# Retention and gated product on one core: 54 matmuls in two halves each, and sums, masks and first products in another order

## The chip, the cores and the metric

One core of a Trainium2 chip. The metric is the time of one execution in microseconds (us). Each kernel is run several times, in rounds with the kernel before on the same chip. Most executions agree within about 1%; a run that is over 1.5% above the fastest of its kernel is called slow and is left out of ratios. A ratio is the mean time of one kernel's fast runs over the mean of the other's fast runs of the same rounds, so it is not quite the ratio of the medians quoted beside it.

## The reference

```python
def reference(q, k, v, w_in, w_out):          # q, k, v: (8, 8, 576, 64)
    scores = q @ k.T / sqrt(64)               # per batch and head
    ret = scores * where(i >= j, gamma[h] ** (i - j), 0)
    x = (ret @ v) -> reshaped to (4608, 512)
    h = x @ w_in                              # (512, 2048)
    g = h * cos(h)
    return g @ w_out                          # (2048, 512)
```

(Shortened; the result is float32, (4608, 512).)

## The kernel before

The tokens are worked through in ten tiles of 512, 256, 256 and seven times 512 rows. In each tile TensorE first makes `h` ("first matmuls", `mm1`: 64 matmuls of 512 columns in tiles 4 to 9), ScalarE and VectorE turn it into `gT`, and then TensorE makes the output from `gT`. From tile 3 on the output is made with seven products instead of eight (Strassen's way), which needs sums `gs` of quarters of `gT`; VectorE (DVE) makes some, GpSimd (POOL) the others. Between these products stand small matmuls of the retention of the next tiles: scores (`sc`), states (`st`), and the parts `cross`, `own` and `same` of `ov`. The chain runs inside a tile: sums of `gs` on VectorE, then the addition `ot` that frees a PSUM bank, then the additions of the states (`s`, `carry`), then ScalarE's copy of the states to `sb`, then the cross matmuls `ov`, which read `sb`.

```python
def g_sum(n, x, e0, e1):
    # ... (which quarters, which operation: cut)
    on_dve = ...  # DVE takes 5, the second half of 2, and (6, first half) in tiles 4 to 8
    i = (nc.vector if on_dve else nc.gpsimd).tensor_tensor(
        out=tiles["gs", n, x][:, e0:e1], in0=i0, in1=i1, op=op_)
    if on_dve:
        tiles["gate"] = i
    elif "gate" in tiles:
        fence(i, tiles.pop("gate"), ...)     # GpSimd's sum waits for the last DVE sum

def sums_after(n, i):
    # ... (tile 3: cut)
    elif n <= CATCH and i in (3, 7):                 # tiles 4 to 7
        for x in (5, 2):
            g_sum(n, x, i - 3, i + 1)
        if i == 7:
            g_sum(n, 6, 0, 4)                        # the third DVE sum
        g_sum(n, 1, i - 3, i + 1)                    # GpSimd from here on
        if i == 7:
            for e in (0, 4):
                g_sum(n, 7, e, e + 4)
            g_sum(n, 6, 4, E2)

def mm2_seven(n, at):                                # the seven products of tiles 3 to 9
    for x in (3, 4, 5, 2, 1, 7, 6):
        # ... (retention of the next tiles at x == 5, 1 and 6: cut)
        parts = product(n, x)
        if x == 3:
            acts.append(lambda: nc.scalar.copy(u22, tiles["all", 3]))
        elif x == 4:
            add(u22, tiles["all", 4], u22)           # "ot": frees the bank of product 4
        # ...
```

## Time and profile before

| | before |
|---|---|
| time, median of 3 runs | 297.47 us (296.58 to 302.08) |
| span of the profiled run | 294.9 us, mean granted TensorE clock 1.0 |
| TensorE (PE) busy | 281.6 us, 95% |
| starts of the first matmuls of tiles 1, 3, 4 to 9 | 50.41, 83.91, 114.84, 145.65, 176.58, 205.96, 236.66, 264.98 us |

TensorE is the bound, so a change pays only where TensorE stands still. One measure is used throughout the rest, read from the trace: the **products stretch** of a tile, from the start of its last first matmul to the start of the next tile's first one. It holds the seven products and the retention matmuls between them, and all waits among these. Before, tiles 4 to 7 took 17.21, 17.34, 15.78 and 17.10 us; where nothing waits it is 15.7 to 15.9 us.

Some of TensorE's waits are put down to "issue": the profile shows nothing that it waits for. Beside them stands what this trace has of the instruction queue (line q8 of its page): 30 packets of 16,384 bytes, for 7,731 records of TensorE (loads, matmuls, its sequencer's), which is 258 records to a packet. The two longest issue waits stand at records 4801 and 6593, 7 x 256 apart. So 256 instructions of TensorE are called a "block" here, and the packet that ended last before TensorE went on is taken for the block's; both are inferred from these places, no line of the profile says so. At five places of this trace (packets ended at 106.18, 111.07, 174.60, 202.33 and 234.61 us) the first instruction behind the wait ran 1.3 to 1.5 us after the packet's end, and 3.4 to 5.2 us (once 8.0) after the first instruction of the block before.

### The profile page before, as it was taken

How to read it: one execution, taken by the hardware profiler on the slowest of the kernel's cores; microseconds unless marked ns; L12 is line 12 of the kernel's file. 1: busy time of each engine (PE TensorE's matmuls, PEld its weight loads, DVE VectorE, ACT ScalarE, POOL GpSimd, SP SyncE). 2: the span in 40 equal slices, each digit the busy share in tenths (PEclk: the TensorE clock that was granted, in tenths of full speed). 3: DMA queues.
4: the chain of work that ended last, by engine and by line, in shares of the span. 5: the costliest groups of instructions: out<-in, count | busy, mean ns of one | idle time of the engine just before them, and what ended most of it. 6: DMA issues, size and time to landing. Idle time of an engine off the chain costs nothing.

```text
span 294.9 us, 8852 instructions
## 1 busy us (share of the span) xinstructions
PE 281.6 (95%) x3850; PEld 190.9 (65%) x3850; DVE 208.0 (71%) x268; ACT 147.8 (50%) x197; POOL 176.7 (60%) x158
## 2 busy tenths in 40 slices
PE   7889999999999999998999979999999899999995
PEld 2568645748568886466746864588458754884594
DVE  5676656576759985788758865797579858945873
ACT  5646434625346545654376526734674567525620
POOL 7482047581192299698497784569566804870583
PEclk9999999999999999999999999999999999999999
DMA  7999999999999998999999999979942240021013
GB/s 217 261 171 194 219 247 251 177 302 235 205 224 215 197 201 205 188 214 175 202 224 232 177 221 203 236 184 218 203 119 39 76 109 0 4 87 57 0 38 108
DMA packets 119031, 50.39 MB, mean 171 GB/s; under 512 B 83024, under 2 KB 117968, under 8 KB 118992
## 3 DMA queue, kind: packets, MB, share of 16 engines
q1 hardware_dynamic: 114224, 45.10, 75.4%
q0 software_dynamic: 4224, 4.19, 8.8%
q8 instruction: 30, 0.49, 0.7%
q10 hardware_dynamic: 544, 0.52, 0.5%
q14 instruction: 9, 0.07, 0.1%
HBM read 36.70 MB, written 9.44 MB: 156 GB/s over the span
## 4 chain that ended last, share of the span: by engine, by line
PE 74%; DMA 9%; DVE 8%; ACT 2%; issue 2%; SPq 2%; POOL 2%; DVEq 0%; PEldq 0%; ACTq 0%
PE h L542 38%; PE o L694 23%; PE o L559 7%; DMA w_out_sb<-in_moe_w_out_dram 6%; PE ov L466 3%; DMA fv<-in_v_dram 3%; PE sc L283 2%; DVE gs L621 2%; DVE s L379 2%; DVE ot L719 2%; SPq L171 1%; DVE ret L295 1%; PE st L356 1%; POOL w_out_sb L965 1%; ACT sb L387 1%
## 5 line engine op out<-in xcount | busy, mean ns | idle before, releaser
L542 PE MATMUL h<-xT,w_in_sb 128*128 128x256 bf16 (+1 forms) x768 | 127.2, 326 | 0.9 <-DVE xT L491 0.8
L621 POOL TENSOR_TENSOR gs<-gT 128x1024 bf16<-128x1024 bf16 x42 | 88.2, 2129 | 62.3 <-DVE gs L621 31.0
L551 DVE TENSOR_TENSOR gT<-h,cosh 128x1024 bf16<-128x1024 f32 x72 | 88.0, 1223 | 46.3 <-ACT cosh L550 46.1
L550 ACT ACTIVATE cosh<-h,half_pi 128x1024 f32<-128x1024 f32 x72 | 80.2, 1114 | 56.2 <-PE h L542 56.2
L542 PEld LDWEIGHTS <-w_in_sb 128*128 128x128 bf16 x768 | 74.6, 98 | 50.8 <-DVE xT L491 1.6
L694 PEld LDWEIGHTS <-gs 128*128 128x128 bf16 x576 | 53.4, 98 | 10.6 <-issue 3.9
L180 POOL TENSOR_TENSOR qs<-fq,gq 128x512 bf16<-128x512 f32 x31 | 32.0, 1063 | 33.2 <-DMA fq<-in_q_dram 33.2
L694 PE MATMUL o<-ws,gs 128*128 128x256 bf16 (+1 forms) x352 | 39.4, 268 | 2.6 <-issue 2.6
L180 POOL TENSOR_TENSOR ks<-fk,gk 128x512 bf16<-128x512 f32 x32 | 34.4, 1090 | 6.1 <-DMA fk<-in_k_dram 5.9
L559 PE MATMUL o<-w_out_sb,gT 128*128 128x512 bf16 x128 | 30.5, 380 | 0.2 <-DMA w_out_sb<-in_moe_w_out_dram 0.2
L387 ACT CAST sb<-s 128x768 bf16<-128x768 f32 (+2 forms) x16 | 10.7, 672 | 34.6 <-DVE s L379 32.2
L719 DVE TENSOR_TENSOR ot<-o,ot 128x512 f32<-128x512 f32 (+2 forms) x32 | 19.7, 621 | 10.2 <-PE o L694 9.6
L694 PE MATMUL o<-w_out_sb,gs 128*128 128x256 bf16 x224 | 25.8, 273 | 0.6 <-DVE ot L719 0.6
L694 PE MATMUL o<-w_out_sb,gT 128*128 128x256 bf16 x224 | 25.8, 273 | 0.0
L491 ACT CAST xT<-ov 128x512 bf16<-128x512 f32 x26 | 15.4, 626 | 19.7 <-PE ov L466 19.7
L694 PEld LDWEIGHTS <-gT 128*128 128x128 bf16 x224 | 21.7, 98 | 4.0
L621 DVE TENSOR_TENSOR gs<-gT 128x1024 bf16<-128x1024 bf16 (+1 forms) x27 | 20.9, 810 | 0.4
L559 PEld LDWEIGHTS <-gT 128*128 128x128 bf16 x128 | 11.5, 98 | 12.7 <-issue 0.5
L719 DVE TENSOR_TENSOR ot<-ot,o 128x512 f32<-128x512 f32 x14 | 9.6, 687 | 7.5 <-ACT ot L749 6.1
L295 DVE TENSOR_TENSOR ret<-sc,tri 128x1024 bf16<-128x1024 f32 x12 | 14.6, 1214 | 0.0
L302 DVE TENSOR_TENSOR ret<-sc,tri 128x1024 bf16<-128x1024 f32 x9 | 10.7, 1219 | 1.8 <-PE sc L283 1.8
L466 PE MATMUL ov<-qT,sb 64*64 64x64 bf16 (+1 forms) x424 | 11.5, 201 | 0.5 <-ACT sb L387 0.2
(88 smaller groups left out, 193.8 us busy)
## 6 DMA issues: line engine op xcount, KB each, us to landing
out_dram<-ot SPq DMA_DIRECT2D x35, 256.0 KB, 3.9
fk<-in_k_dram SPq DMA_DIRECT2D x23, 256.0 KB, 6.7
fv<-in_v_dram SPq DMA_DIRECT2D x23, 256.0 KB, 4.9
fk<-in_k_dram SPq DMA_DIRECT2D x4, 512.0 KB, 7.6
fv<-in_v_dram SPq DMA_DIRECT2D x4, 512.0 KB, 8.1
w_in_sb<-in_moe_w_in_dram POOLq DMA_DIRECT2D x4, 512.0 KB, 7.4
w_out_sb<-in_moe_w_out_dram POOLq DMA_DIRECT2D x4, 512.0 KB, 13.1
fq<-in_q_dram SPq DMA_DIRECT2D x4, 512.0 KB, 6.5
```

What stands on the lines that cost most here:

```text
L180: eng.tensor_tensor(out=out_.rearrange("p (b a) d -> p a b d", a=2), in0=f.rearrange("p (a b) d -> p a b d", a=2), in1=by.rearrange("p (a ...
L295: nc.vector.tensor_tensor(out=ret, in0=ps, in1=by, op=ALU.mult)
L387: run(sb[:, :n], s32[:, :n])
L466: i = nc.tensor.matmul(dst if name == "own" else as_queries(G, dst), lhsT=lhsT, rhs=rhs, start=at not in begun, stop=left[at] == 0, skip_g ...
L491: (evacs or (evac, evac))[x](xT[:, x], ps)
L542: nc.tensor.matmul(ps[:, j, :], lhsT=w_in_sb[:, dg, (et + j) * P : (et + j + 1) * P], rhs=xT[:, dg], start=(dg == 0), stop=(dg == DG - 1),)
L550: nc.scalar.activation(cosh, ps, ACTF.Sin, bias=half_pi, scale=1.0)
L551: nc.vector.tensor_mul(gT[:, et : et + m, c0 : c0 + w], ps, cosh)
L559: nc.tensor.matmul(ps, lhsT=gT[:, et, tsi * P : (tsi + 1) * P], rhs=w_out_sb[:, et, :], start=(et == 0), stop=(et == ET - 1),)
L621: i = (nc.vector if on_dve else nc.gpsimd).tensor_tensor(out=tiles["gs", n, x][:, e0:e1], in0=i0, in1=i1, op=op_)
L694: nc.tensor.matmul(dst[i], lhsT=lhs[:, e, j * P : (j + 1) * P], rhs=rhs[:, e, c0:c1], start=(x in (3, 4, 1, 7) and e == 0 and (i == 0 or l ...
L719: pend.append(lambda: nc.vector.tensor_tensor(out=out_, in0=in0, in1=in1, op=op_))
```

## The change

Its intent: to close the places where TensorE waits. One VectorE sum of tiles 4 to 7 goes behind the addition that frees a bank; half a cast and some matmuls of the start are placed otherwise; masks of tile 2 come behind an evacuation that the next tile waits for; and 54 first matmuls of tile 5 are made in two halves, which computes nothing new but shifts every later instruction. Cut to the lines that change:

```diff
+    halves = {S7 + 2: 54}                       # tile 5
     def mm1(n, et, c0, w, bank, inside={}):
-                nc.tensor.matmul(ps[:, j, :], lhsT=..., rhs=xT[:, dg],
-                    start=(dg == 0), stop=(dg == DG - 1))
+                parts = [slice(0, w)]
+                if halves.get(n, 0):
+                    halves[n] -= 1
+                    parts = [slice(0, w // 2), slice(w // 2, w)]
+                for part in parts:
+                    nc.tensor.matmul(ps[:, j, part], lhsT=..., rhs=xT[:, dg, part],
+                        start=(dg == 0 and part.start == 0),
+                        stop=(dg == DG - 1 and part.stop == w), skip_group_check=True)

     def sums_after(n, i):                       # the moved sum
-            if i == 7:
-                g_sum(n, 6, 0, 4)
     def mm2_seven(n, at):
             elif x == 4:
                 add(u22, tiles["all", 4], u22)
+                if S7 < n <= CATCH:
+                    pend.append(lambda: g_sum(n, 6, 0, 4))

-    nc.gpsimd.tensor_copy(tiles["v", 1], tiles["fv", 1])          # the start
+    nc.gpsimd.tensor_copy(tiles["v", 1][:, :HG], tiles["fv", 1][:, :HG])
+    nc.scalar.copy(tiles["v", 1][:, HG:], tiles["fv", 1][:, HG:])
-    load(2, gates=(w_dma[4], w_dma[5]))
+    load(2, gates=(w_dma[4],))
-        next(planes1)()                         # second pair's scores: out of state1 ...
-                (0, 0): {2: state1},
+                (0, 0): {1: lambda: next(planes1)(), 3: state1},
-                        part1("cross", True), part1("own"), part1("same"), ...
+                        part1("own"), part1("same", True), part1("cross"), ...
-            bank = {0: "nmnm", ...                                # three outputs side by side
+            bank = {0: ("n", "st", "m", "n"), ...
-            order[: 2 * ET] = ... for t in range(2) ...
+            order[: 3 * ET] = ... for t in range(3) ...           # banks of carry, begin: n -> m

-        banks = {..., 3: "abmabmab"}                              # tile 2
+        banks = {..., 3: "mabmabma"}
-                (24, lambda: [masked() for masked in scores(5)]),
-                (24, lambda: end(both)),
+                (24, lambda: masks2.extend(scores(5))),
+                (24, lambda: (end(both), masks2.pop(0)(), masks2.pop(0)())),
```

More of the change, by code (lines that the diff above doesn't have):

```diff
@@ L541, in mm1 @@
             for dg in range(DG):
-                nc.tensor.matmul(
-                    ps[:, j, :],
-                    lhsT=w_in_sb[:, dg, (et + j) * P : (et + j + 1) * P],
-                    rhs=xT[:, dg],
-                    start=(dg == 0),
-                    stop=(dg == DG - 1),
-                )
+                parts = [slice(0, w)]
[3 more added lines that the diff above has]
+                for part in parts:
+                    nc.tensor.matmul(
+                        ps[:, j, part],
+                        lhsT=w_in_sb[:, dg, (et + j) * P : (et + j + 1) * P],
+                        rhs=xT[:, dg, part],
+                        start=(dg == 0 and part.start == 0),
+                        stop=(dg == DG - 1 and part.stop == w),
+                        skip_group_check=True,
+                    )
         cosh = cosp.tile([P, m, w], F32, tag="cosh", name="cosh")
@@ L555, in mm2 @@
         if et == 0:
-            bank = {0: "nmnm", 1: "nm", 2: "mn"}[n][tsi]
+            bank = {0: ("n", "st", "m", "n"), 1: "nm", 2: "mn"}[n][tsi]
             tiles["o", tsi] = psum.tile([P, DM], F32, tag=bank, name="o")
@@ L1071 @@
                 blocks = [(e + k * E2, 0, w) for e in range(0, E2, m) for k in range(2)]
-        banks = {0: "mbmabmab", 1: "abma", 2: "bmab", 3: "abmabmab"}.get(n, "abmabmab")
+        banks = {0: "mbmabmab", 1: "abma", 2: "bmab", 3: "mabmabma"}.get(n, "abmabmab")
         for i, (et, c0, cw) in enumerate(blocks):
             inside = {
-                (0, 0): {2: state1},
+                (0, 0): {1: lambda: next(planes1)(), 3: state1},
                 (0, 1): {
                     0: lambda: (
-                        part1("cross", True), part1("own"), part1("same"), first_[0][1](*both)
+                        part1("own"), part1("same", True), part1("cross"), first_[0][1](*both)
                     ),
@@ L1107 @@
                 (48, lambda: masks2.pop(0)()),
-                (51, lambda: (carry((2,), ("n", "st")), masks2.pop()())),
-                (58, lambda: begin(2, ("n", "st"))),
+                (51, lambda: (carry((2,), ("m", "st")), masks2.pop()())),
+                (58, lambda: begin(2, ("m", "st"))),
                 (61, lambda: end(both)),
@@ L1166 @@
             part = 3 * ET // 4
-            order[: 2 * ET] = [(t, e) for e in range(part) for t in range(2)] + [
-                (t, e) for t in range(2) for e in range(part, ET)
+            order[: 3 * ET] = [(t, e) for e in range(part) for t in range(3)] + [
+                (t, e) for t in range(3) for e in range(part, ET)
             ]
```

## The prediction

> **What bounds the kernel now.** I read the profile's page first, then TensorE's own waits, the chain that ended last, the timeline around every wait, the instruction queue's DMA packets, and VectorE's sums beside GpSimd's. The page's head:
>
> ```profile
> span 294.9 us, 8852 instructions
> PE 281.6 (95%) x3850; PEld 190.9 (65%) x3850; DVE 208.0 (71%) x268; ACT 147.8 (50%) x197; POOL 176.7 (60%) x158
> PE 74%; DMA 9%; DVE 8%; ACT 2%; issue 2%; SPq 2%; POOL 2%; DVEq 0%; PEldq 0%; ACTq 0%
> q8 instruction: 30, 0.49, 0.7%
> ```
>
> TensorE is busy 95% at full granted clock and holds 74% of the chain. Nothing in the change removes TensorE work, so it can only gain where TensorE stands still: 294.9 - 281.6 = 13.3 us, of which 3.5 us lie before 15.3 us and 3.6 us after 291 us, where the change touches nothing. TensorE's waits, by what ended them:
>
> ```profile
> PE o L694 <- issue: 2.6, 2, 1.5
> PE h L542 <- DVE xT L491: 0.8, 2, 0.6
> PE st L356 <- POOL vb L1016: 0.7, 1, 0.7
> PE o L694 <- DVE ot L719: 0.6, 1, 0.6
> PE o L559 <- DMA w_out_sb<-in_moe_w_out_dram: 0.2, 1, 0.2
> ```
>
> Each of these five lines has a piece of the diff aimed at it. The largest, 2.6 us, is "issue": TensorE waits for nothing that the profile shows, once 1.53 us (at 174.60 in the chain in order of time) and once 1.07 us (at 234.81).
>
> [...] The trace: 30 packets of 16,384 bytes on the instruction queue. Counting TensorE's records (loads, matmuls, its sequencer's own), the first long issue wait stands at instruction 4801 and the second at 6593, exactly 7 x 256 apart; the packets before them ended at 174.60 and 234.61. So these two waits are late blocks[...]; an instruction runs some 1.3 to 1.5 us after its block's packet ended (also at 107.67, 112.51 and 203.86, where waits of 0.15 to 0.3 us stand). [...] 64 of 512 columns in 13.81 us are 216 ns each, 104 of 256 columns in 11.46 us are 110 ns. [...]
>
> ```profile
> 251.52 2.13 POOL L621 TENSOR_TENSOR gs<-gT 128x1024 bf16<-128x1024 bf16 x1
> 253.08 1.73 DVE L621 TENSOR_TENSOR gs<-gT 128x1024 bf16<-128x1024 bf16 x2
> ```
>
> GpSimd's sum ends at 253.65; the first of the two DVE sums ends at 254.20, 0.55 us after it, where the undisturbed sum takes 0.69.
>
> **The change, part by part.**
>
> *a) Start.* Half of the cast of the second v goes to ScalarE (GpSimd's whole cast: 16.00 to 17.03). The state matmuls move behind 12 of the 16 first matmuls, so their wait of 0.71 us for that cast goes. Three outputs side by side put 36 instead of 24 matmuls (12 x 0.216 = 2.6 us more) ahead of the last quarter of w_out; its wait of 0.22 us goes. TensorE is thus some 0.9 us ahead at 38 us. But from 20 to 50 us the DMA engines are full (busy share 1.21 in the table by stretches) and the keys of the third pair set the next step: their GpSimd scaling runs from 41.35 to 42.91, and the transposes start at 42.96. What TensorE gained would be waited away there, unless data come sooner. They do by as much as GpSimd issues the remaining weights earlier, half of its cast, 0.5 us. The lifted gate on the load of k does nothing: q stands before it on the same queue and is not through until 39. **-0.5 us.**
>
> *b) Tile 2.* VectorE now does the evacuation before the two masks of the fifth pair:
>
> ```profile
> 80.86 2.35 DVE L302 TENSOR_TENSOR ret<-sc,tri 128x1024 bf16<-128x1024 f32 x2 [1.31 <-PE sc L283]
> 83.14 0.72 DVE L491 CAST xT<-ov 128x512 bf16<-128x512 f32 x1
> 83.91 1.92 PE L542 MATMUL h<-xT,w_in_sb 128*128 128x256 bf16 x16 [0.58 <-DVE xT L491]
> ```
>
> The xT would be ready at about 82.35. The eight output matmuls before it began at 81.43, the next could follow at 81.43 + 8 x 0.216 = 83.16 instead of 83.91. The new order of PSUM banks (the first block in m) keeps the masks out of its way. **-0.75 us.**
>
> *c) The sum of tiles 4 to 7.* One DVE sum (0.69 us) goes behind the addition that frees a bank for the fourth product. In tile 4 that addition made TensorE wait 0.61 us. But GpSimd's chain of four sums (2.1 us each) is fenced behind the last DVE sum issued before it. With that sum moved, GpSimd starts 0.6 us sooner, [...] and the moved sum comes while GpSimd's first one runs. Tile 5 before:
>
> ```profile
> 162.07 1.90 DVE L621 TENSOR_TENSOR gs<-gT 128x1024 bf16<-128x1024 bf16 x3
> 163.88 0.69 DVE L719 TENSOR_TENSOR ot<-o,ot 128x512 f32<-128x512 f32 x1
> 164.48 0.42 DVE L379 TENSOR_TENSOR s<-st,carry 128x256 f32<-128x256 f32 x1
> ```
>
> After: two sums to 163.36, GpSimd 163.44 to 165.55, the addition 163.3 to 164.0, the moved sum blocked until 165.55 + 0.55 = 166.1, the states from 166.0 instead of 164.48: 1.5 us late. The chain goes on through ScalarE's copies (165.85 to 166.99 before) to the cross matmuls of the pair (167.28), with 0.3 us of slack: TensorE would wait 1.2 us. Tiles 6 and 7 have the same spacing, 1.2 us each; tile 4 has no slack (its cross matmuls at 137.52 wait for that copy already): 1.5 us, and the 0.61 us are not saved but waited away. **+5.1 us** if nothing absorbs it; **-0.6** if the moved sum slips in first.
>
> *d) 54 matmuls in halves.* 2 x 110 against 216 ns: 54 x 4 ns = **+0.2 us**; the 54 more weight loads (98 ns) fit beside 110 ns matmuls. They compute nothing new, so their use must be another: they put 108 instructions in front of everything from tile 5 on and shift every block boundary there by 108. Both issue waits lie behind them. The two boundaries move out of the places where they stall; new ones fall into the dense parts of tiles 5 and 6 (5 and 2.6 us apart there[...]). Both waits gone would be -2.6; with about 0.8 back in new ones, **-1.8 us**.
>
> Sum with the full cost of c: -0.5 - 0.75 + 5.1 + 0.2 - 1.8 = +2.2, so 299.7 us; some of it absorbed, because a wait at the cross matmuls also gives a late block time to come (another 0.8): 299. Without it: -0.5 - 0.75 - 0.6 + 0.2 - 1.8 = -3.5, so 294.0.
>
> **Rivals.** *The lock on tiles 4 to 7 decides* (299 us): for it speak the seven overlaps in the trace, all ending 0.54 to 0.56 us after GpSimd; against it, that somebody kept this order. *Instruction blocks decide* (292.5 to 294): for it, the distance of exactly 7 x 256 and the number 54, which looks found by trial on the chip; against it, that one late block (174.60) was [...] served 4.7 us after its predecessor began, in a burst of loads, which a shift need not cure. *The start passes fully* (another -0.4): if k of the third pair does come sooner. *Nothing arrives* (297.5): each gain becomes a wait for the next thing on an engine that is behind; the DMA is not such a thing after 225 us, where its share falls to 0.5.
>
> **Range and chances.** The mechanism says 299, the look of a number that was searched for says 294; I give both the same weight: 296.5 us. The range goes from 292.5 (all waits gone, no lock) to 300.5 (lock in full and a new late block). Faster by over 2% would be under 291.5 us, more than all the waits that the change is aimed at: 0.07. Slower by over 2% would be over 303.4: 0.04. Within: 0.89.
>
> **What would show it.** a) No wait of TensorE on the cast of v at 17 us nor on w_out, first tile-1 matmul 0.5 us earlier than 50.41, a wait at the key transposes near 42.5. b) Masks behind the evacuation, no wait of h on xT. c) In tiles 4 to 7 a DVE sum of over 1.5 us that ends 0.55 us after GpSimd's, and ov waiting on sb. If it takes 0.69 us there or ov waits for nothing, the step is wrong. d) Issue waits at other instruction counts, again multiples of 256 apart, and fewer; if 1.5 us of issue stands in tile 5 again, it was the burst of loads and not the place. The prediction is wrong if the time falls outside the range, and its mechanism is wrong if it is near 294 with the lock paid.

## The result, and the profile after

| | before | after |
|---|---|---|
| time, median | 297.02 us (295.74 to 302.08, 4 runs) | 301.06 us (300.1 to 301.88, 4 runs) |
| ratio of the fast runs | | 1.015, 95% interval 1.0103 to 1.0198 |
| products stretch, tiles 4 to 7 (profiled run) | 17.21, 17.34, 15.78, 17.10 | 17.16, 17.29, 18.68, 17.41 |

The kernel is 1.5% slower. The time is 0.56 us above the predicted range. The head of the page after, its chain and its clock row:

```profile
span 300.0 us, 8938 instructions
PE 281.7 (94%) x3881; PEld 197.5 (66%) x3904; DVE 212.2 (71%) x268; ACT 148.0 (49%) x198; POOL 178.8 (60%) x158
PEclk9979999999999999999999999999999999999999
PE 77%; DVE 12%; DMA 3%; issue 2%; ACT 2%; POOL 2%; DVEq 0%; PEldq 0%; POOLq 0%; ACTq 0%
```

TensorE is as busy as before (281.7 against 281.6 us), so the 5.1 us of span are waits. DVE is busy 4.2 us longer with the same 268 instructions and holds 12% of the chain, where it held 8%. TensorE's waits after (us in total, times, longest):

```profile
PE ov L466 <- ACT sb L387: 3.7, 4, 0.9
PE h L549 <- DMA w_in_sb<-in_moe_w_in_dram: 2.2, 1, 2.2
PE o L700 <- issue: 1.4, 1, 1.4
PE sc L283 <- DVE ret L295: 1.0, 4, 0.3
```

The waits for the cast of `v` and for `w_out` are gone, as intended, and so is that of the fourth product for `ot`. In their place stands `ov <- sb`, four times 0.93 us, once in each of tiles 4 to 7. The groups of the sums, first before, then after (duration ns min/median/max), show where it comes from:

```profile
L621 DVE TENSOR_TENSOR gs<-gT x27: 678/691/1524, 96.6 to 282.7; 128x1024 bf16<-128x1024 bf16 x26, 128x2048 bf16<-128x2048 bf16 x1
```

```profile
L629 DVE TENSOR_TENSOR gs<-gT x27: 677/691/2232, 98.2 to 287.9; 128x1024 bf16<-128x1024 bf16 x26, 128x2048 bf16<-128x2048 bf16 x1
```

The longest sum has grown from 1.5 to 2.2 us. The timeline of tile 5 after (start, us, engine, line, operation) shows the chain:

```profile
164.06 1.29 DVE L629 TENSOR_TENSOR gs<-gT 128x1024 bf16<-128x1024 bf16 x2
165.27 0.68 DVE L725 TENSOR_TENSOR ot<-o,ot 128x512 f32<-128x512 f32 x1
165.43 6.74 POOL L629 TENSOR_TENSOR gs<-gT 128x1024 bf16<-128x1024 bf16 x3 [1.97 <-DVE gs L629]
165.87 2.23 DVE L629 TENSOR_TENSOR gs<-gT 128x1024 bf16<-128x1024 bf16 x1
168.02 0.41 DVE L379 TENSOR_TENSOR s<-st,carry 128x256 f32<-128x256 f32 x1
169.38 0.83 ACT L387 CAST sb<-s 128x768 bf16<-128x768 f32 x1 [5.40 <-DVE s L379]
170.26 0.56 PE L466 MATMUL ov<-qT,sb 64*64 64x64 bf16 x16 [0.92 <-ACT sb L387]
```

GpSimd's first sum is released by the second DVE sum, two where there were three, and starts at 165.43. The moved sum starts 0.44 us later and takes 2.23 instead of 0.69 us; in the trace GpSimd's first sum ends at 167.55, and the moved sum at 168.10. The states follow it, `sb` follows them, and the cross matmuls wait. In tiles 4, 6 and 7 the same: 2.23 us each time, its end 0.54 us behind that of GpSimd's. What step c of the prediction describes, a moved sum that ends only after GpSimd's and holds up the states, is thus seen; what holds the sum is not shown. Of step d a part is seen in this profile: two issue waits of 2.6 us in all became one of 1.4 us, where the prediction left 0.8. It is a late instruction block again, now in tile 6 (from the start of the last matmul before it at 204.31 to the next at 205.95; the block's packet on the instruction queue ended at 204.52).

The w_in wait of 2.2 us at the start, and the half clock in the third slice that follows it, are not the change's alone: the kernel before shows the same wait in a later profile (below), and the run b_tile2, which has the old start, shows both. In this pair of profiles they weigh much: tile 1 starts 2.63 us later than before, tile 2 gives 0.74 us back, the products stretches of tiles 4 to 7 take 3.11 us more (67.43 and 70.54 in all) and the halved first matmuls 0.13 us; together tile 8 starts 5.15 us later. The timed runs differ in the same way: two of the four have a mean clock of 0.994 (one window of half clock, as explained below) and took 301.70 and 301.88 us; two have 0.998 and took 300.10 and 300.41 us, inside the predicted range.

### The profile page after: what moved, and what is told of

It reads as the page before. It is cut to its first block, busy times and chain, and to the rows that moved or that the text cites.

```text
span 300.0 us, 8938 instructions
## 1 busy us (share of the span) xinstructions
PE 281.7 (94%) x3881; PEld 197.5 (66%) x3904; DVE 212.2 (71%) x268; ACT 148.0 (49%) x198; POOL 178.8 (60%) x158
## 4 chain that ended last, share of the span: by engine, by line
PE 77%; DVE 12%; DMA 3%; issue 2%; ACT 2%; POOL 2%; DVEq 0%; PEldq 0%; POOLq 0%; ACTq 0%
PE h L549 41%; PE o L700 22%; PE o L567 8%; PE ov L466 3%; DVE gs L629 3%; DMA w_in_sb<-in_moe_w_in_dram 3%; DVE s L379 2%; DVE ret L295 2%; DVE ot L725 2%; PE sc L283 1%; PE st L356 1%; POOL tri L937 1%; DVE carry L379 0%; DVE xT L491 0%; ACT sb L387 0%
## 5 line engine op out<-in xcount | busy, mean ns | idle before, releaser
L629 POOL TENSOR_TENSOR gs<-gT 128x1024 bf16<-128x1024 bf16 x42 | 90.0, 2172 | 71.5 <-PE h L549 36.0
L549 PEld LDWEIGHTS <-w_in_sb 128*128 128x128 bf16 x822 | 80.2, 98 | 47.3 <-DMA w_in_sb<-in_moe_w_in_dram 2.4
L180 POOL TENSOR_TENSOR ks<-fk,gk 128x512 bf16<-128x512 f32 x32 | 33.7, 1067 | 4.7 <-DMA fk<-in_k_dram 4.7
L567 PE MATMUL o<-w_out_sb,gT 128*128 128x512 bf16 x117 | 28.4, 379 | 1.2 <-issue 1.0
L629 DVE TENSOR_TENSOR gs<-gT 128x1024 bf16<-128x1024 bf16 (+1 forms) x27 | 26.2, 993 | 0.4
L295 DVE TENSOR_TENSOR ret<-sc,tri 128x1024 bf16<-128x1024 f32 x12 | 14.5, 1212 | 0.0
L466 PEld LDWEIGHTS <-sb 64*64 64x64 bf16 x424 | 7.5, 106 | 9.7 <-ACT sb L387 5.3
```

The costliest lines, as they stand in the source:

```text
L180: eng.tensor_tensor(out=out_.rearrange("p (b a) d -> p a b d", a=2), in0=f.rearrange("p (a b) d -> p a b d", a=2), in1=by.rearrange("p (a ...
L295: nc.vector.tensor_tensor(out=ret, in0=ps, in1=by, op=ALU.mult)
L466: i = nc.tensor.matmul(dst if name == "own" else as_queries(G, dst), lhsT=lhsT, rhs=rhs, start=at not in begun, stop=left[at] == 0, skip_g ...
L549: nc.tensor.matmul(ps[:, j, part], lhsT=w_in_sb[:, dg, (et + j) * P : (et + j + 1) * P], rhs=xT[:, dg, part], start=(dg == 0 and part.star ...
L567: nc.tensor.matmul(ps, lhsT=gT[:, et, tsi * P : (tsi + 1) * P], rhs=w_out_sb[:, et, :], start=(et == 0), stop=(et == ET - 1),)
L629: i = (nc.vector if on_dve else nc.gpsimd).tensor_tensor(out=tiles["gs", n, x][:, e0:e1], in0=i0, in1=i1, op=op_)
```

## The experiments

By "lock" is meant what step c describes: the VectorE sum does not end until GpSimd's has ended (in the kernel after, in each of tiles 4 to 7, 0.54 us behind it, after 2.23 us where 0.69 is usual). A "late block" is a block of 256 instructions that TensorE has to wait for, as read above. By how much it is late, and how long TensorE "stands", is counted from the start of the last matmul before to the start of the next; the waits in the lines of a profile are 0.2 to 0.4 us shorter, because they count from that matmul's end.

The theory to test after this result: the moved sum's lock costs some 5 us, start and tile 2 give about 1 us back, and the halves do nothing. The rival: the halves cost as well. In the names of the runs, `a_` starts from the kernel after, `b_` from before, `good_` from start and tile 2 of the change alone.

### One part undone, one part alone

**The sum put back** in the kernel after:

```diff
+            if i == 7:
+                g_sum(n, 6, 0, 4)
-                if S7 < n <= CATCH:
-                    pend.append(lambda: g_sum(n, 6, 0, 4))
```

> The changed kernel with the one VectorE sum of tiles 4 to 7 put back in front of the addition, the rest of the change kept. [...] (the moved sum is blocked by GpSimd's first sum and delays the states): the sum takes 0.69 us again, the wait of ov on sb of about 1.2 us in each of four tiles goes, about -4.5 us against the changed kernel, so 296 to 297 us, a ratio to before of 0.995 to 1.0. Start theory (the loss comes from the 2.2 us wait for the first weights): the time stays near 301. Block theory (the shift of the instruction blocks brings new late blocks): the time stays near 300, with issue waits of over 1 us.

Measured: 303.37 us median (298.17 to 307.01, two of four runs slow) against 298.48 for before; ratio 1.0099, interval 0.994 to 1.0258. The lock is gone (the sum takes 0.69 us again, `ov` waits for nothing in tiles 4 to 7), and yet the time is not better. TensorE now stands still at late instruction blocks: 2.45 us in tile 3, 2.09 in tile 5, 2.73 in tile 6. Products stretches of tiles 5 and 6: 19.00 and 19.70 us. (The block in tile 3 stands in front of everything that this run puts back.) The ratio alone is not clear of 1; the median, with the slow runs, is 1.6% above.

**The sum moved, nothing else** (the same diff reversed, in the kernel before):

> The kernel before with only that sum moved. [...] a VectorE sum of about 2.2 us in tiles 4 to 7, ending 0.54 us after GpSimd's, ov waiting about 1.2 us for sb in each; 4 x 1.2 = 4.8 us, less the wait of 0.6 us in tile 4 and less what a late block had cost anyway (up to 2.6): 299 to 301.5 us, ratio 1.008 to 1.015. Start and block theories: no change, ratio 1.00.

Measured: 303.53 us against 298.48; ratio 1.0187, interval 1.008 to 1.0295. `ov` waits for `sb` 3.6 us in four times. The moved sum alone is enough for a loss, but not all of this one is the sum's: the profiled run also has a block 2.3 us late in tile 3, in front of every moved sum, with half a clock behind it, and one 1.3 us late in tile 7. Its tiles 4 to 7 took 70.15 us. The lock by itself is measured further below.

**Halves taken out** of the kernel after (`halves = {}`):

> The changed kernel with all matmuls of tile 5 whole. If halves only shift the instruction blocks: the blocks fall at other places from tile 5 on, the wait of 1.4 us in tile 6 goes or moves, and the time is within 1.5 us of 301 either way. If halves cost TensorE time by themselves, it is faster by more than the 0.2 us worked out from 110 against 216 ns.

Measured: 301.44 us against 298.48; ratio 1.0134, interval 1.0046 to 1.0222. The lock's waits are there as in the kernel after. Against the 1.015 of the kernel after, on another chip, taking the halves out changes nothing that can be told from zero.

**GpSimd's sums behind the moved one**, so that the moved sum slips in before them:

```diff
             g_sum(n, 1, i - 3, i + 1)           # now only for i == 3; those of i == 7 go below
-            if i == 7:
-                for e in (0, 4):
-                    g_sum(n, 7, e, e + 4)
-                g_sum(n, 6, 4, E2)
                     pend.append(lambda: g_sum(n, 6, 0, 4))
+                    # and behind it: (1, 4, E2), (7, 0, 4), (7, 4, E2), (6, 4, E2)
```

> The changed kernel with the sum moved as there, but GpSimd's four sums issued after it and fenced behind it[...]. [...] the sum takes 0.69 us and the time is that of the kernel with the sum put back, 296 to 297 us, although the order of VectorE's work is the changed one; the risk is that GpSimd's sums end 1.3 us later and the seventh product waits for them, up to 0.5 us a tile. Order theory (the place of the sum in VectorE's own order costs the time, not GpSimd): it stays near 301.

Measured: 303.14 us against 298.48; ratio 1.0175, interval 1.0082 to 1.0267. The lock's waits are gone but for 0.37 us in tile 4. Again late blocks came: 3.82 us in tile 5, 1.69 in tile 6.

So far: with the lock, a loss; without it, late blocks and, by the medians, a loss of the same order. Either undone alone is no cure that these runs show. That asked for the other parts alone, and for both undone together.

**The halves alone**, in the kernel before:

```diff
+    halves = {S7 + 2: 54}
```

> The kernel before with the 54 halves alone. Theory of the prediction: the halves only move the places of the instruction blocks behind tile 4; the block boundaries at instructions 4801 and 6593 of TensorE, where the profile before shows 1.8 and 1.3 us of standing still (from 174.3 and from 234.5 us), then fall 108 instructions earlier in the work. If both waits go and none comes, -2.9 us; if the places only change, 0. The halves themselves cost 0.2 us. The sums of tiles 5 to 7 stay at 0.69 us each and ov waits for nothing. From the four runs so far (late blocks came wherever the lock's wait did not give the fetch time) I expect -0.5 us, between -2 and +2, and waits of 1 to 3 us at other block boundaries. Rival: the splitting itself costs more than 0.2 us (weight loads that 110 ns matmuls do not hide): then tile 4, where all 54 halves are, is longer by over 0.5 us.

Measured: 302.44 us (300.49 to 304.19) against 296.7; **ratio 1.0186, interval 1.0124 to 1.0247**. The halves alone cost as much as the sum alone. My expectation of -2 to +2 us was wrong (it also calls the tile with the halves tile 4; it is tile 5). Its rival can be settled from the trace: the stream of first matmuls with 54 halves takes 13.73 us instead of 13.60, here and in every other run that has them, so splitting itself costs 0.13 us. TensorE's waits in this run:

```profile
PE ov L466 <- issue: 2.8, 1, 2.8
PE o L702 <- issue: 2.6, 1, 2.6
PE o L567 <- DMA w_out_sb<-in_moe_w_out_dram: 1.5, 1, 1.5
```

Two waits for nothing that the profile shows, in tile 5 (from 174.24) and tile 6 (from 203.69). Their blocks' packets on the instruction queue, worked out from the trace as in the prediction (boundaries 256 instructions apart):

```
tile 6            block began   next block's packet   next block wanted   used
before              198.83       201.04 to 202.33          203.7         203.86
with halves         201.13       203.93 to 205.23          203.69        206.61
```

In both, the packet starts 2.2 to 2.8 us after its predecessor came into use and takes 1.3 us, and the block is used 1.4 to 1.5 us after the packet's end: 5.0 to 5.5 us in all. Before, TensorE needed 4.9 us for the 256 instructions between, so the block came almost in time. With the halves the boundaries stand elsewhere, the block between them holds the small matmuls of the retention, and TensorE was through in 2.6 us. So the halves moved the boundaries out of a good place in tile 6 into a bad one. In tile 7 they did the opposite: 15.86 us instead of 17.10.

And there is a second loss behind such a wait. The table of stretches (us; then the busy times of PE, PEld, DVE, ACT, POOL; then the granted clock, the DMA share and GB/s) around the wait in tile 6:

```profile
193.40:203.60 10.20, 10.20 (x261) 8.88 (x259) 8.63 (x14) 5.64 (x10) 7.68 (x5) 1.00 0.74 176
203.60:206.70 3.10, 0.45 (x5) 0.17 (x3) 2.15 (x4) 1.10 (x3) 3.10 (x3) 0.91 1.18 215
206.70:210.20 3.50, 3.50 (x19) 2.41 (x19) 0.69 (x1) 0.00 (x0) 3.50 (x5) 0.59 0.62 174
210.20:213.00 2.80, 2.69 (x74) 2.34 (x74) 1.38 (x2) 0.59 (x1) 2.80 (x4) 1.00 0.88 191
```

Behind 2.9 us of standing still TensorE is granted half its clock: the trace records one window from 206.15, 3.41 us long, just before TensorE goes on. More on this below.

**Tile 2 alone** and **the start alone** (their hunks of the diff above):

> The kernel before with the new order of tile 2 alone (evacuation before the masks of the fifth pair, first block of tile 3 in bank m). Theory: the wait of 0.58 us of h on xT goes, tile 3 starts 0.6 us sooner after tile 2's start (33.5 us before, 32.9 with it, as in the profile after), and the rest follows: -0.6 us. Rival: the gain is waited away later (at the sums of tiles 4 to 7 or at late instruction blocks): 0.

Measured: 295.9 us against 296.7; ratio 0.9986, interval 0.9926 to 1.0045: too little to be told in the time. In the trace it is plain: from the first matmul of tile 1 to that of tile 3 it takes 33.50 us before and 32.75 here (32.76 in the kernel after).

> The kernel before with the four changes of the start alone (split cast of v, lifted gate, new order of the pair's scores, own and cross parts, three outputs side by side). Theory: no wait of TensorE on the cast of v at 17 us, none on w_out; first matmul of tile 1 at 49.9 us instead of 50.4 (-0.5), with a wait of up to 0.8 us at the key transposes near 42.5. The profile after had it at 53.0 because its first w_in load was issued 1.3 us late; I hold that for chance, so here and in most runs it should not come. Rival: the new order itself delays the weights: then tile 1 starts after 51.5 us here as well.

Measured: 295.89 us against 296.7; ratio 0.9961, interval 0.9894 to 1.0027. Tile 1 starts at 50.27 us against 50.41 in the first profile before, so the rival (a delay by the new order) is not seen in this trace; whether 0.5 us are gained only more traces can say (below).

**Start and tile 2 together**, sum and halves left out:

> The kernel after without the moved sum and without the halves: the start and tile 2 alone. Theory: sums of tiles 4 to 7 at 0.69 us with no wait of ov on sb beyond what tile 4 had before; the late blocks stand at the same instructions as before, give or take the few that the start adds (at about 174 and 234 us). -1.1 us if nothing else comes. Rival, from the first four runs on a noisier chip: the time set free at one place is waited away at late blocks: 0 to -0.3.

Measured: 295.83 us against 296.7; ratio 0.9953, interval 0.9898 to 1.0008. With both undone, the loss is gone.

### What the halves do, and where

**128 halves, one whole block more**, in the kernel before: `halves = {S7 + 1: 64, S7 + 2: 64}`.

> The kernel before with all 128 first matmuls of tiles 4 and 5 in halves: 256 more instructions, exactly one block, in front of the products of tile 5. The block boundaries inside tiles 5, 6 and 7 stand at the same matmuls as in the kernel before; only those of tile 4 differ, by 128. Theory 'place': splitting costs 128 x 4 ns = 0.5 us and no more; tiles 5, 6 and 7 take from the last first-matmul to the next tile what they take before (15.6 to 17.3, 15.8 and 17.1 us), not the 18.6 and 19.9 us of the run with 54 halves. Time +0.5 us, between -1 and +1.5. Rival 'splitting': the halves themselves are what cost: then 128 of them cost 2.4 times the 5.7 us of 54.

Measured: 302.27 us (two of four runs slow) against 296.81; ratio of the fast runs 1.0117, interval 1.0022 to 1.0211. Tiles 6 and 7 behave as the theory says: 15.74 and 17.10 us, as before. Tiles 4 and 5 do not: 20.40 and 21.06 us, with blocks 2.99 and 3.88 us late, whose packets started 5.1 and 5.4 us after their predecessors came into use. The profiled run is one of the slow ones. The expectation for the time was missed; that splitting itself costs little is read from the streams of first matmuls, 13.86 and 14.07 us with 64 halves each (the second begins in a window of half clock).

**The halves in tile 7**, with start and tile 2: `halves = {CATCH: 54}`.

> Start and tile 2 of the change, its sum left where it was, and the 54 halves in tile 7 instead of tile 5. Theory 'place': tiles 4 to 6 keep the places of before (16.6, 15.6 to 17.3 and 15.7 us from the last first-matmul to the next tile), and tile 7 gets the place that it had with the halves in tile 5, 15.9 instead of 17.1 us: -1.2 + 0.2. With start and tile 2: 1 us under the same without halves, so some 2 us under before. Rival: the gain in tile 7 was not the place but that tiles 5 and 6 were late: then tile 7 stays at 17 us.

Measured: 294.64 us against 296.81; ratio 0.9953, interval 0.9887 to 1.0018. The profiled run has a span of 291.6 us, the shortest of all, with stretches of 15.76, 15.88, 15.76 and 15.87 us: nothing waits in tiles 4 to 7. Tile 7 has the 15.9 us predicted for this place.

**The load of v later**, with the halves:

```diff
+    halves = {S7 + 2: 54}
     def prep_inside(n, i):
-                    load(G + 2)
+                    load(G + 2, "k")
     def feed(s):
         if r == 0:
+            if G + 2 < NP:
+                load(G + 2, "v")
```

> The kernel before with the 54 halves, and the load of the even pair's v in tiles 4 to 7 issued after the first output store of the tile instead of right behind q and k. In the run with the halves the fetch of a block in tile 5 began 5.2 us after its predecessor came into use (elsewhere in dense parts some 2 us), while the issue of that v load stood on the sync queue for 4.7 us, and TensorE stood still for 3.0 us. Theory 'burst': without that load in the way the fetch begins within 3 us and tile 5 loses 1.5 to 3 us of its late block; tile 6, whose block is only 2.3 us long (the place itself), keeps its 2.5 to 3. Time 1.5 to 3 us under the run with halves alone. Rival: the place alone decides and the loads do not matter: 0.

Measured: 300.76 us against 296.81; ratio 1.0145, interval 1.0086 to 1.0205, which overlaps that of the halves alone. The block in tile 5 was 2.55 us late, its packet started 4.6 us after its predecessor came into use (5.2 in the run with the halves). The theory that this one load holds the fetch up falls. Over all traces, the fetches of blocks that came over 1 us late started 3.0 to 5.9 us after their predecessors came into use in tile 5, 2.9 to 4.7 us in tile 3 and 1.4 to 2.8 us in tile 6. Why they differ so stays open.

**Sum and halves together**, without start and tile 2: both diffs in the kernel before.

> The kernel before with the moved sum and the 54 halves and nothing else. Alone the sum cost 1.9% and the halves 1.9%. If the two costs add: +11 us. Theory: they do not, because the lock's wait at the cross matmuls lets the late block of tile 5 arrive (in the kernel after, tile 5 took 17.3 us with both, 18.6 to 21 with the halves alone, 17.2 with the lock alone): tile 4 +0, tile 5 +0, tile 6 +2.9, tile 7 +0.3 as in the profile after: +3 to +5.5.

Measured: 304.37 us against 296.81; ratio 1.0251, interval 1.0173 to 1.0329. The two costs, 1.9% each by themselves, come to less than 3.7% together, though by the intervals of the three ratios that is not certain. The trace shows how they can hide each other. With the lock TensorE waits 1.2 us at the cross matmuls of tiles 5 to 7 (2.0 in tile 4), and the block in tile 6 that was 2.9 us late with the halves alone is 0.5 us late: its predecessor begins just behind that wait and lasts 3.1 us instead of 2.6, and the packet starts 0.8 instead of 2.8 us after the predecessor's first instruction.

**The halves in tile 8**, in the kernel before: `halves = {CATCH + 1: 54}`.

> The kernel before with the 54 halves in tile 8, behind which every part has room (tile 8's products took 14.7 us at every place of the block boundaries so far). A control for the run with 128 halves, which was to show that splitting is cheap but lost 3 to 4 us twice at late blocks in tiles 4 and 5. Theory 'place': +0.2 us and nothing else, so 0.997 to 1.005 times before; the 54 split matmuls lengthen the stream of first matmuls of tile 8 by 0.2 us. Rival 'splitting': +1% or more as in the other runs with halves on the kernel before.

Measured: 298.49 us against 296.23; ratio 1.0068, interval 1.0023 to 1.0114. More than the 0.2 us of splitting, and the profile shows where: blocks late by 1.2 us in tile 3 and 2.4 us in tile 5, in front of every halved matmul, and one window of half clock in tile 6. As a control this is not clean: the interval excludes 1, and nothing in this kernel explains a loss in front of tile 8. before_again below shows how far such blocks move by themselves. The rival that splitting itself costs is out by the stream of first matmuls of tile 8, 13.73 instead of 13.60 us.

**The halves in tile 6**, in the kernel before: `halves = {S7 + 3: 54}`.

> The kernel before with the 54 halves in tile 6: tile 5 keeps the block boundaries of before, tile 6 gets those that it had with the halves in tile 5 (11 instructions behind the first product, the next 256 on), tile 7 as well. Theory 'place': tile 6 takes 19 to 20 us from the last first-matmul to the next tile instead of 15.7, with a wait of 2.5 to 3 us in the first product behind the second half of the cross matmuls; tile 7 takes 15.9 instead of 17; tile 5 stays at 15.6 to 17.4. Sum +2.3 us. Rival: tile 6 was late only because tile 5 was late before it (the loads and fetches shifted): then tile 6 stays near 16.

Measured: 299.11 us against 296.23; ratio 1.0117, interval 1.0069 to 1.0165. Tile 6: 17.15 us with a block 1.6 us late, in the first product behind the cross matmuls as expected, though not as late as expected; tile 7: 15.87 us. Here too blocks were late in front of every half: 2.3 us in tile 3 and 2.2 us in tile 5, so only a part of the time belongs to the halves.

### The lock by itself

The kernel after with its halves in tile 7 (`halves = {CATCH: 54}`) has the lock at the quiet places. Beside it ran good_halves7 once more, which is the same kernel without the moved sum:

> The kernel after with its 54 halves in tile 7 instead of tile 5, everything else as in it: the moved sum at the places of the blocks that had no late block (the same places as in the run without the moved sum, where tiles 4 to 7 took 15.8, 15.9, 15.8 and 15.9 us). So this measures the lock by itself. Theory: 1.2 to 1.5 us in each of tiles 4 to 7, each 17.0 to 17.4 us, +5 to +5.5 us against that run, some +3.5 us against before (1.2%). Rival: a good part of the lock's wait is hidden and the loss of the change is its late blocks: then under +2.5 us against that run.

> Start and tile 2 of the change, its sum left where it was, the 54 halves in tile 7: the candidate once more with more rounds, beside the others on the same chip, because its first interval (0.9887 to 1.0018) touches 1. Expected 0.993, between 0.988 and 0.998: 2 us under before, with tile 7 near 15.9 us again.

Measured on one chip: 299.71 us for the first, ratio 1.0152 (interval 1.0106 to 1.0199); 296.37 us for the second, ratio 1.000 (0.9962 to 1.0038); the intervals do not touch. The lock alone thus makes a difference of 1.5%, 4.5 us. From the last matmul before to the first `ov` that waits for `sb` it takes 1.2 us in tiles 5, 6 and 7 and 2.1 us in tile 4. The timeline of tile 5 without the moved sum (good_halves7), against the one shown above:

```profile
161.36 1.90 DVE L629 TENSOR_TENSOR gs<-gT 128x1024 bf16<-128x1024 bf16 x3
163.17 0.68 DVE L727 TENSOR_TENSOR ot<-o,ot 128x512 f32<-128x512 f32 x1
163.33 6.30 POOL L629 TENSOR_TENSOR gs<-gT 128x1024 bf16<-128x1024 bf16 x3 [2.50 <-DVE gs L629]
163.77 0.41 DVE L379 TENSOR_TENSOR s<-st,carry 128x256 f32<-128x256 f32 x1
165.14 0.83 ACT L387 CAST sb<-s 128x768 bf16<-128x768 f32 x1 [3.85 <-DVE s L379]
166.59 0.32 PE L466 MATMUL ov<-qT,sb 64*64 64x64 bf16 x16
```

Here GpSimd starts behind all three DVE sums. The states follow the addition at once, at 163.77, `sb` is ready at 165.97, and `ov` begins at 166.59 without a wait. The second result is a disappointment in another way: as a version to beat before, good_halves7 is not established (0.9953 and 1.000 in two batches).

### How much is the run and not the kernel

> The kernel before, unchanged, once more: how far the late blocks of one and the same kernel move from run to run. The run with the halves in tile 8, which leaves every instruction of TensorE in front of tile 8 as it was, was 0.7% slower than before, with late blocks of 1.2 us in tile 3 and 2.4 us in tile 5 (0.3 and 1.8 in the first profile) and one window of half clock. If such places are a matter of the run: ratio 1.000 within 0.4%, but late blocks in tiles 3 and 5 that differ by 0.5 us or more from the first profile. Rival: one kernel's late blocks repeat within 0.3 us; then what the halves in tile 8 lost is something that they do to the whole program.

Measured: 296.17 us (20 runs) against 295.48 (27 runs); ratio 1.0015, interval 0.9987 to 1.0043: the comparison is sound. But the waits of one and the same kernel are not the same twice. TensorE's waits of this profile:

```profile
PE h L542 <- DMA w_in_sb<-in_moe_w_in_dram: 2.2, 1, 2.2
PE ov L466 <- issue: 0.8, 1, 0.8
PE o L694 <- issue: 0.5, 1, 0.5
```

The 1.5 us of issue in tile 5, on which the prediction's step d stood, is not there (the tile's stretch is 15.83 instead of 17.34 us); the wait for w_in is, which the first profile did not have; in tile 7 a block is 0.8 instead of 1.3 us late.

> The kernel after, unchanged, beside the two best-known numbers: with the halves moved to tile 7 it was 1.0152 times before. Theory: with the lock paid (1.2 us of ov waiting on sb in each of tiles 4 to 7) the place of the halves matters little: 1.013 to 1.018, no window of half clock behind 30 us, since its waits stay under 2 us. Rival: the place of the halves costs with the lock too: 1.02 or more.

Measured: 301.06 us (6 runs) against 295.48; ratio 1.0207, interval 1.0157 to 1.0257. Stretches of 17.15, 17.69, 17.16 and 17.41 us. With the halves in tile 7 the same lock gave 1.0152; the intervals overlap, so neither theory of that expectation is excluded, but the late block in tile 6 (1.63 us in the first profile after) did not come back.

### The clock behind a long wait

All twenty traces together hold 36 places between 30 and 285 us where more than 1.2 us passed from the start of one matmul to the start of the next. Eighteen lasted 1.27 to 1.87 us; none was followed by a lower clock. Eighteen lasted 2.04 to 3.88 us; twelve of them were followed, within 5 us, by one window of half clock, 3.41 us long each time (two windows began up to 0.5 us before TensorE went on). There were no other such windows in that part of any trace. What separates the twelve from the six can be read from the same traces. Every window begins a whole number of steps of 3.413 us after the point where the trace's clock first reached full: 4 steps in the kernel after (full from 4.76 us, the window of 3.413 us from 18.41), 39 in a_no_halves, 59 in b_halves; in the first profile before the full clock lasts 290.13 us, 85 steps. Cut into such steps, the twenty traces have 1590 between 10 and 285 us. In sixteen of them matmuls were busy 11 to 41% of the step, and a window followed all sixteen; in the others they were busy 47% or more, and none followed. So in these traces waits of like length cost a window or not by how they fall on the steps: in b_halves the 2.92 us from 203.69 left 36% of a step busy, the 2.98 us from 174.24 left 47%. In the run with the halves in tile 8 one of them fell into the stream of first matmuls, which took 15.19 instead of 13.60 us: 1.6 us for one window. The mean clock of a timed run counts them, wherever they stand (0.994 is one window in 300 us): before_again's 11 runs without one took 295.4 us in the mean, its 6 fast runs with one 296.6. The kernels with halves in tile 5 and no lock have one to four of them in every timed run (b_halves 1, 1, 3, 1; a_sum_back 2, 2, 4, 2).

## Why the prediction was wrong, point by point

- **a) Start, -0.5 us: not shown.** The waits on the cast and on w_out are gone. In the traces without the w_in wait tile 1 starts at 50.25 to 50.91 us with the new start (six traces, mean 50.51) and at 50.41 to 51.71 with the old one (seven, mean 51.03; b_sum_halves, with another wait of 2.3 us at 16 us, is left out). The difference is the size predicted, but the spread is larger, and the first profile before was at its low end. Over all ten traces of each kind, those with such waits included, nothing is left of it: means of 51.37 and 51.40 us. The wait at the key transposes near 42.5 that the prediction asked for shows in good_halves7_5 (0.96 us from 42.52) and in a_sum_back (0.84), but b_sum_moved, with the old start, has one of 0.67. The wait for w_in came in four of ten traces with the new start and in two of ten with the old; whether the new start makes it likelier is open, and both profiles of the kernel after have it, with a window of half clock behind. The prediction had no such wait in its range: in these two profiles tile 1 starts at 53.04 and 53.31 us.
- **b) Tile 2, -0.75 us: right.** 33.50 to 32.76 us.
- **c) The moved sum, +5.1 us with the lock in full: right in what happens, and in size for tiles 5 to 7; tile 4 was priced too high.** Why the sum is held is not shown; that it is, the trace before showed, and the runs do. The moved sum takes 2.23 us and ends 0.54 us behind GpSimd's (predicted 0.55); TensorE waits 1.2 us in each of tiles 5 to 7. On quiet places it makes 1.5%, 4.5 us. Over tiles 4 to 7 the second profiles of both kernels differ by 4.7 us (69.4 against 64.7). In tile 4, for which the prediction put 1.5 us, the lock adds nothing in the first pair and 0.6 us in the second: 17.21 and 16.54 us before, 17.16 and 17.15 after. The prediction overlooked that two DVE sums of this tile were blocked in the first profile before already (1.45 and 1.52 us from 131.26, ending 0.55 and 0.54 us after work on GpSimd); in both profiles of the kernel after they take 0.69. That the whole comes near 5.1 on quiet places is therefore luck in part: there tile 4 had no old wait (15.76 us in good_halves7).
- **d) Halves, +0.2 and -1.8 us: the -1.8 is the step of the sum that failed.** The +0.2 was right (0.13 measured). It rests on 216 and 110 ns, the means of two streams of the trace before (64 matmuls of 512 columns in 13.81 us, 104 of 256 columns in 11.46 us). "The two boundaries move out of the places where they stall; new ones fall into the dense parts of tiles 5 and 6", it said, and put 0.8 us on the new ones. By themselves the halves cost 1.86%, 5.5 us: in the profile TensorE stands 2.98 and 2.92 us at the new places in tiles 5 and 6, with a window of half clock behind the second, and only tile 7 gains (1.2 us). Beside the lock they cost little, but they gain nothing either: tiles 4 to 7 took 70.15 us with the moved sum alone (b_sum_moved), and 70.54 and 69.41 in the two profiles of the kernel after. In tiles 5 to 7, where c put 3.6 us and d -1.8, the two pairs of profiles differ by 3.2 and 4.1 us instead of 1.8. The waits that d wanted to win were in part gone with c: the late block of tile 5 is in neither trace with the lock and no halves (17.18 us in both). The prediction's remark that a wait at the cross matmuls also gives a late block time to come was the right thought, applied to 0.8 us where it held more. And of the 2.6 us of issue waits that were to be won, 1.5 are not there in every run. That the gain is missing in the time of the kernel after as well fits the runs, but is not clear of their noise: 1.015 with the halves and 1.0134 without, on two chips.
- **The weighing.** The full-cost sum was 299.7 us. With the shift of blocks at 0 instead of -1.8 it would have been 301.5; measured 301.06 twice. This is a fit made afterwards: in the first pair of profiles c and d together came to 3.2 us, near the 3.5 of that sum, because the overpriced tile 4 and the missing gain of d offset each other, and what went beyond the sum there was the start. The prediction gave half its weight to 294 because a number that looks searched for should pay. Nothing in the trace spoke for that; the seven overlaps in the trace spoke for the lock. The rival "instruction blocks decide" was half right: they decide, but against the change.

## What to carry to other kernels

A sum moved behind an addition took three times its length here (2.23 us instead of 0.69), with GpSimd's sums fenced to those left in front of it, so that they started first. Moving the fence with it took the waits away here (a_pool_behind); that it pays is not shown, since that run had the halves in tile 5. Where two waits hide each other, undoing one part at a time makes each look harmless (here 1.0099, not clear of 1, and 1.0134, against 0.9953 with both undone on another chip): try each part alone in the old kernel too. A late instruction block seen in one profile is no fixed quantity (in tile 5 of the kernel before 1.8 us in one profile and none in the other); look at a second profile of the same kernel before pricing its removal, and reckon that a wait of over 2 us may cost more than its length: twelve of eighteen here brought a window of half clock, some 1.6 us where TensorE is dense.
